# Packed attention with a gated layer on one core: w_out's first quarters loaded earlier, two output chunks started inside batch 0's h, output matmuls between batch 1's packed blocks

## The chip, the core and the metric

The kernel runs on one core of a Trainium2 chip. The metric is the device time of one execution in microseconds (us). All times below are of the kernel before the change, from three timed executions and one profiled execution with its trace.

The engines go by their profile names: PE (matmuls; PEld loads its weights), DVE (VectorE), ACT (ScalarE), POOL (GpSimd) and SP (SyncE). POOL and SP here mostly issue DMAs. Each engine works through its own instructions in program order and waits on semaphores of the others.

## The reference

```python
def _attn_ref(q, k, v, p):          # 8 batches, 8 heads, 576 tokens, head size 64; 32 packed queries p
    scale = 1.0 / np.sqrt(q.shape[-1])
    def sm_attn(qq, kk, vv):
        s = scale * np.matmul(qq, kk.transpose(0, 1, 3, 2))
        s = s - np.max(s, axis=-1, keepdims=True)
        a = np.exp(s)
        a = a / (np.sum(a, axis=-1, keepdims=True) + 1e-09)
        return np.matmul(a, vv)
    p_packed = sm_attn(p, k, v)
    return sm_attn(q, p_packed, p_packed)

def _moe_ref(x, w_in, w_out):       # x: 4608 x 512, w_in: 512 x 2048, w_out: 2048 x 512
    h = x @ w_in
    g = h * np.cos(h)
    return g @ w_out
```

The packed queries p attend to k and v; q attends to the result; the heads are joined to x, and x goes through the layer with w_in, h times cos(h), and w_out.

## The kernel before

One batch (576 tokens) after the other goes through these steps, and the steps of neighbouring batches are interleaved by an order written out by hand.

- `load` (L103) brings q, k or v of a batch, cast to bf16, by a DMA that POOL issues; `load_w_in` and `load_w_out` (L403, L407) bring a quarter of each weight matrix. POOL issues them in order, and at most eight are under way: the ninth waits until the first has landed.
- q and k are transposed, for batches 0 and 1 (and k of 2) by PE (`pe_T`, L119), later by DMAs on SP's queue (`xbar`, L111).
- `s1` (L160): scores of p and k on PE, exp on ACT, giving a1. a1 is transposed by PE (`a1_pe`, L181) or by a DMA on SP's queue (`a1_xbar`, L176), and `pp` (L191) multiplies it with v; `pp_T` (L206) transposes that to ppT.
- `s2` (L239): scores of q and pp, exp on ACT giving a2u; `sums2` (L246) sums on PE and takes Ln on ACT; `normalise` (L256) takes Exp on ACT and multiplies on DVE, giving a2n.
- `ppw` (L213): pp times w_in for 512 columns of w_in, the "packed block": eight matmuls on 64 rows and 32 columns of the array (L225). Four blocks make PPW of a batch. ACT and DVE copy them out, one bank each.
- h is a2n times PPW. It is made in 16 chunks of 128 of the 2048 columns. For batches 0 and 1, `h_one` (L295) makes 512 tokens of a chunk in one PSUM bank with two matmuls (L301); ACT takes the cosine (L306), DVE multiplies (L307) into gT. The last 64 tokens of eight chunks are made together by `h_half` (L310), which writes the tile joint. From batch 2 on, `h_mm` (L268) does all 576 tokens.
- The output: for each chunk of 128 tokens, 16 matmuls of gT with w_out accumulate in one bank (L365; for batch 0, L378), and `store` (L355) copies it to SBUF and has SP store it. These output matmuls are the filler: `fill(n)` (L395) emits the next n of them wherever the order says so. `out_first` (L371) gives the order for batch 0. It begins with the four matmuls on w_out's first quarter for each of the four chunks 0 to 3, and it keeps chunks 2 and 3 in two extra banks (psX).

PSUM has eight banks here. Two (pool O) hold output chunks. The other six are cut up in four ways (`banks`, L56): "pairs" are three tiles of two banks; "held" is psX with two banks, and two pairs; "single" is a ring of six single banks, H0 to H5, from which `one` (L115) takes the next by the counter `turn`; "four" is a ring of four single banks beside psX. When output chunk 3 of batch 0 is stored, `out_first` calls `banks("single")` and sets the counter: the ring then covers all six, psX's two as H0 and H1.

`slot(1, ...)` (L519, called at L563) is the h of batch 1: after each of the 16 chunks it emits its share of output matmuls (`weight`) and runs the hooks that stand at that chunk: the half chunks, transpositions on SP's queue, batch 1's fourth packed block.

The loads of later batches are tied to events by `behind` (L107): a POOL instruction that reads one element of a tile, so that what POOL issues after it waits until that tile is written.

Of the kernel before, what the change touches and what calls it, by code (L numbers as in the profile page):

```python
# [9 lines left out]
BF16 = mybir.dt.bfloat16  # L10
# [5 lines left out]
def kernel(  # L16
# [39 lines left out]
    def banks(kind):  # L56


        inner.close()
        if kind != "four":  # L60
            outer.close()
        for name, n, st in {"held": [("psX", 2, outer), ("psA", 1, inner)], "four": [("psH", 1, inner)],
                            "single": [("psH", 1, inner)]}.get(kind, [("psB", 1, inner), ("psA", 1, inner)]):
            psum[name] = st.enter_context(tc.tile_pool(name=name, bufs=n, space=PSUM, reuse_waits="tile"))
        pairs[:], turn[0] = (["A0", "A1"] if kind == "held" else ["A0", "A1", "B"]), 0
        ring[0] = 4 if kind == "four" else 6
        if kind in ("four", "single"):
            for i in range(ring[0]):
                psum["psH"].tile([128, 512], FP32, name="psH", tag=f"H{i}")
# [22 lines left out]
    def copy(eng, out, in_):  # L92
        if eng is ACT:
            ACT.copy(out=out, in_=in_)  # L94
        else:
            eng.tensor_copy(out=out, in_=in_)  # L96
# [10 lines left out]
    def behind(t):  # L107

        G.tensor_copy(out=gate, in_=t)  # L109
# [103 lines left out]
    def ppw(b, n, eng=None, own=None, later=False, cuts=((0, 512),)):  # L213
        if b not in PPW:
            PPW[b] = ppw_pool.tile([128, 2, DF], BF16, name="PPW", tag="PPW")
        two = isinstance(eng, tuple)
        if own:
            ps = [own(), own()]
        else:
            t = psa()  # L220
            ps = [t[:, 0, :], t[:, 1, :]]
        for x in range(4):
            for y in range(2):
                r = slice(64 * y, 64 * y + 64)
                nc.tensor.matmul(ps[y][32 * x:32 * x + 32, :], ppT[b % 2][r, 0, x, :],  # L225
                                 w_in_bf[r, x, n * 512:(n + 1) * 512], start=True, stop=True)

        def evacuate(cuts=cuts):
            if own or two:
                for a, z in cuts:  # L230
                    for y in range(2):
                        copy(eng[y] if two else eng, PPW[b][:, y, n * 512 + a:n * 512 + z], ps[y][:, a:z])
            else:
                copy(eng or (V, ACT)[n % 2], PPW[b][:, :, n * 512:(n + 1) * 512], t)
        if later:
            return [lambda c=c: evacuate((c,)) for c in cuts]
        evacuate()

    def s2(b):  # L239
# [67 lines left out]
            return lambda: V.tensor_tensor(out=gT[b][:, fc, 0:512], in0=ps, in1=cs, op=ALU.mult)  # L307
        return cos

    def h_half(b, a):  # L310

        t = one()
        for f in range(8):
            fc = 8 * a + f
            for y in range(2):
                nc.tensor.matmul(t[:, f * 64:f * 64 + 64], PPW[b][:, y, fc * 128:(fc + 1) * 128],  # L316
                                 a2n[b][:, y, 512:576], start=(y == 0), stop=(y == 1))
        cs = cos_pool.tile([128, 512], BF16, name="cosT")
        ACT.activation(out=cs, in_=t, func=AF.Sin, bias=PI_HALF)
        j0 = (b % 2) * 64  # L320
        V.tensor_tensor(out=joint[b // 2][:, 8 * a:8 * a + 8, j0:j0 + 64], in0=t.rearrange("p (f x) -> p f x", x=64),
                        in1=cs.rearrange("p (f x) -> p f x", x=64), op=ALU.mult)
# [46 lines left out]

    def out_first():  # L370

        pss = {}
        for c, fcs in ((0, 4), (1, 4), (2, 4), (3, 4), (0, 8), (1, 8), (2, 8), (3, 8),
                       (2, 12), (3, 12), (2, 16), (3, 16), (0, 16), (1, 16)):
            if c not in pss:
                pss[c] = (O if c < 2 else psum["psX"]).tile([128, DM], FP32, name="ot", tag="ot")
            for fc in range(8 if (c, fcs) in ((0, 16), (1, 16)) else fcs - 4, fcs):
                nc.tensor.matmul(pss[c], gT[0][:, fc, c * 128:(c + 1) * 128], w_out_bf[:, fc, :],  # L378
                                 start=(fc == 0), stop=(fc == NFC - 1))
                if fc == NFC - 1:  # L380
                    store(0, c, pss[c], V if c == 2 else ACT)
                    if c == 3:
                        banks("single")
                        turn[0] = 3
                yield

    filler = []

    def set_filler(b):
        filler.append([out_gen(b) if b else out_first(), 16 * n_chunks(b)])  # L390
# [12 lines left out]
    def load_w_in(n):  # L403
        G.dma_start(out=w_in_bf[:, :, n * 512:(n + 1) * 512],
                    in_=moe_w_in.rearrange("(a p) n -> p a n", p=128)[:, :, n * 512:(n + 1) * 512])

    def load_w_out(n):  # L407
        G.dma_start(out=w_out_bf[:, n * 4:(n + 1) * 4, :],
                    in_=moe_w_out.rearrange("(a p) n -> p a n", p=128)[:, n * 4:(n + 1) * 4, :])
# [15 lines left out]
    load("k", 1)  # L425
    for n in range(3):
        load_w_in(n)
    wz = const.tile([128, 512], BF16, name="wz")
    V.memset(wz, 0.0)
    wz4 = const.tile([128, 512], FP32, name="wz4")  # L430
# [21 lines left out]
    warm(1)  # L452
    pp_T(0)
    pe_T("q", 0, (V, ACT, V))
    load_w_out(0)
    load("q", 1)
    for n in range(1, 4):
        load_w_out(n)
    G.dma_start(out=p_raw[:, 4:, :], in_=p_rows[:, 4:, :])
    load("k", 2)  # L460
# [12 lines left out]
    cut_ppw()  # L473
    rest_ppw()
    banks("single")
    a1_pe(1, own=one)
    recips(1)
    for fc in range(13):
        h_one(0, fc)()()
        if fc in (0, 4, 8):  # L480
            ppw(0, 1 + fc // 4, (ACT, ACT if fc == 8 else V), own=bank)
    c13 = h_one(0, 13)
    pp(1, ACT, own=bank)
    c13()()
    c14 = h_one(0, 14)
    c15 = h_one(0, 15)
    pp_T(1, ACT, own=bank)
    c14()()
    c15()()
    set_filler(0)  # L490
    fill(4)
    for n, at in ((0, 2), (1, 0), (2, 4)):
        turn[0] = at
        if n == 2:
            fill(4)
            ACT.preload_act_table_set(EXP_SET)
        ppw(1, n, (ACT, V), own=one)
    banks("held")
    t = psa(BF16)
    for i in range(2):  # L500
        pe_T("q", 1, (None,) * 3, (i,), own=lambda dt: t[:, i, :])
    V.tensor_copy(out=xT["q", 1][:, 0:16].rearrange("p (i a) x -> p i (a x)", i=2), in_=t[:, :, 0:8 * TP])
    pe_T("q", 1, (V, V, ACT), (2,), own=lambda dt: psum["psX"].tile([128, 1024], dt, name="ot", tag="ot"))
    fill(4)
    load("k", 3)
    load("q", 2)
# [4 lines left out]
    sums2(1, 0)  # L511
    fill(2)
    sums2(1, 1)
    fill(9)
    normalise(1)
    ACT.preload_act_table_set(SIN_SET)
    fill(4)
# [40 lines left out]
    def cross(n, b):  # L558
        return lambda: xbar(n, b)

    osb_eng[0] = ACT
    banks("four")
    slot(1, [(5, lambda: h_half(0, 0)), (6, cross("k", 3)), (6, lambda: h_half(0, 1)),  # L563
             (7, lambda: ppw(1, 3, (ACT, V), own=one)), (9, cross("q", 2)), (9, lambda: h_half(1, 0)),
             (10, lambda: pack_p(2, 4, one(BF16))), (11, lambda: h_half(1, 1)), (12, tk2),
             (13, lambda: pe_T("k", 2, (None, None, V), (2,), own=one))],
         trail=8, heavy={5: (0, 1), 6: (0, 1), 7: (0, 1), 9: (0, 1), 11: (0, 1)},
         weight=[3, 3, 3, 4, 4, 2, 2, 2, 3, 2, 2, 2, 1, 2, 3, 3])
    banks("pairs")
    ACT.preload_act_table_set(EXP_SET)  # L570
    osb_eng[0] = V
    behind(xT["q", 2][0:1, 0, 0:1])
    load("v", 3)
    load("q", 3)
    load("k", 4)

    fill(4)
    s1(2)
# [6 lines left out]
    pp(2)  # L585
    s1(3)
    a1_xbar(3)
    fill(2)
    pp_T(2)
    recips(3)  # L590
# [13 lines left out]
    nc.sync.dma_start_transpose(out=P2[:, 4:B].rearrange("p b (t h) n -> p (b t) (h n)", t=2),  # L604
                                in_=p_bf[:, 8:2 * B].rearrange("p g t d -> p (g t d)"))
    behind(xT["k", 4][0:1, 0, 0:1])
    for n, b in (("v", 4), ("q", 4), ("k", 5)):
        load(n, b)
    fill(9)
    osb_eng[0] = ACT  # L610
    slot(2, [(7, lambda: tiled(2))], 0, {7: (6, 4)}, lambda: pp_T(3, V))
# [1 line left out]
    for s in range(3, B):  # L613
        nxt = s + 1 < B
        ACT.preload_act_table_set(EXP_SET)
        osb_eng[0] = V
        if s % 2:
            set_filler(s - 1)
        fill(5)
        s2(s)  # L620
        ppw(s, 0, V)
        fill(8 if nxt else 9)
        if nxt:
            s1(s + 1)
            ppw(s, 1, V)
            a1_xbar(s + 1)
            xbar("q", s + 1)
            recips(s + 1)
            if s + 2 < B:
                xbar("k", s + 2)  # L630
                behind(xT["k", s + 2][0:1, 0, 0:1])
        else:
            for n in range(1, 4):
                ppw(s, n, V)
        fill(4 if nxt else 5)
        sums2(s, 0)
        fill(5)
        sums2(s, 1)
        normalise(s)
        ACT.preload_act_table_set(SIN_SET)  # L640
        fill(13)
        osb_eng[0] = ACT
        for n, b in (("v", s + 2), ("q", s + 2), ("k", s + 3)):
            if b < B:
                load(n, b)
        if nxt:
            slot(s, [(7, lambda: tiled(s))], 0 if s % 2 else 1, {7: (5, 4)}, lambda: pp_T(s + 1, V),
                 7 if s % 2 else 0)
        else:
            slot(s, [], trail=7)  # L650
# [32 lines left out]
```

## Time and profile before

| | us |
|---|---|
| median of three executions (lowest, highest) | 244.16 (244.12, 244.28) |
| profiled execution, its own time | 244.22 |
| its span, first to last instruction | 242.4 |
| PE busy in the span | 232.9 |
| ACT, DVE, POOL busy | 166.5, 162.8, 36.2 |
| output matmuls (L365, L378, 128x512), mean of one | 0.38 |
| DMA queue of the loads (q0): moved | 18.75 MB |

How to read it: the span is what the trace covers, and the rest of the execution's time lies around it. A matmul's busy time is longer than the distance to the next, since matmuls overlap in the array, so a busy PE isn't yet PE at its peak. In the timeline, a row gives the start, the time from the first start to the last end, the engine, the line, the operation with output and inputs, the count, and in brackets the idle time of the engine ahead of it with what ended it. Rows of the same kind are merged. In the list of waits the three numbers are the total, the number of times and the longest.

### The profile page before, as it was taken

The numbers are of one execution on the slowest core, as the hardware profiler recorded it, in microseconds if no ns is written. First come the engines' busy times: TensorE is split into PE (matmuls) and PEld (weight loads), VectorE is DVE, ScalarE is ACT, GpSimd is POOL, SyncE is SP. The second block draws the span as 40 slices with busy tenths as digits, with TensorE's granted clock in tenths as the row PEclk, the third lists the DMA queues.
The fourth block names the chain that finished last, engine by engine and source line by source line (L and its number), as shares of the span: only waits on it lengthen the run. The fifth ranks groups of instructions, "written<-read, shape, count | busy, mean of one in ns | idle before, by whom it ended". The sixth has DMA issues, their size and how long they took to land.

```text
span 242.4 us, 5480 instructions
## 1 busy us (share of the span) xinstructions
PE 232.9 (96%) x2244; PEld 126.0 (52%) x2244; DVE 162.8 (67%) x261; ACT 166.5 (69%) x268; POOL 36.2 (15%) x58
## 2 busy tenths in 40 slices
PE   7789899999999999999999999999999999999994
PEld 3454244456445564556546554556456554565453
DVE  3259993688558786687857686777758787877001
ACT  2349899688659778876878677867787683776110
POOL 8522212200300005000500311030100110010000
PEclk9999999999999999999999999999999999999999
DMA  6999999999999999999999999989285101311133
GB/s 96 203 205 206 206 206 225 201 235 201 175 133 162 197 183 166 211 179 179 186 209 225 184 191 208 191 160 213 66 161 119 46 0 46 87 43 46 47 83 87
DMA packets 64376, 37.37 MB, mean 154 GB/s; under 512 B 36864, under 2 KB 59776, under 8 KB 64352
## 3 DMA queue, kind: packets, MB, share of 16 engines
q0 software_dynamic: 23152, 18.75, 51.7%
q1 hardware_dynamic: 40960, 18.16, 37.1%
q8 instruction: 17, 0.28, 0.5%
q10 hardware_dynamic: 240, 0.13, 0.2%
q14 instruction: 7, 0.06, 0.1%
HBM read 37.22 MB, written 9.44 MB: 192 GB/s over the span
## 4 chain that ended last, share of the span: by engine, by line
PE 83%; DMA 8%; DVE 4%; ACT 2%; issue 1%; POOLq 0%
PE ot L365 42%; PE psA L275 17%; PE ot L378 6%; DMA a1T<-a 5%; PE psH L301 4%; DMA kbf<-in_k_dram 3%; PE psA L155 2%; PE psA L225 2%; PE psA L251 2%; PE psA L198 1%; PE ot L348 1%; DVE gT L307 1%; DVE PPW L96 1%; PE psA L128 1%; PE psH L316 1%; DVE a2n L261 1%
## 5 line engine op out<-in xcount | busy, mean ns | idle before, releaser
L365 PE MATMUL ot<-w_out_bf,gT 128*128 128x512 bf16 x448 | 114.8, 379 | 0.0
L282 DVE TENSOR_TENSOR gT<-psA,cosT 128x576 bf16<-128x576 f32 x96 | 71.4, 757 | 16.3 <-ACT cosT L279 15.3
L279 ACT ACTIVATE cosT<-psA 128x576 bf16<-128x576 f32 x96 | 62.4, 652 | 21.3 <-PE psA L275 20.0
L275 PE MATMUL psA<-a2n,PPW 128*128 128x288 bf16 x384 | 62.7, 286 | 0.0
L365 PEld LDWEIGHTS <-gT 128*128 128x128 bf16 x448 | 42.1, 98 | 38.2 <-issue 4.2
L275 PEld LDWEIGHTS <-PPW 128*128 128x128 bf16 x384 | 37.5, 98 | 25.4 <-issue 0.6
L96 DVE CAST PPW<-psA 128x1024 bf16<-128x1024 f32 x19 | 23.0, 1220 | 7.9 <-PE psA L225 7.9
L307 DVE TENSOR_TENSOR gT<-psH,cosT 128x512 bf16<-128x512 f32 x32 | 21.0, 688 | 4.5 <-ACT cosT L306 4.4
L96 DVE COPY osb<-ot 128x512 f32<-128x512 f32 (+2 forms) x18 | 11.7, 649 | 16.1 <-PE ot L348 14.6
L306 ACT ACTIVATE cosT<-psH 128x512 bf16<-128x512 f32 x32 | 18.5, 615 | 4.6 <-PE psH L301 3.5
L94 ACT COPY osb<-ot 128x512 f32<-128x512 f32 (+1 forms) x20 | 11.4, 568 | 14.8 <-PE ot L365 12.2
L261 DVE SCALAR_TENSOR_TENSOR a2n<-a2u,r,lns 128x576 bf16<-128x576 bf16 x16 | 12.4, 815 | 12.4 <-ACT lns L259 12.4
L301 PE MATMUL psH<-a2n,PPW 128*128 128x512 bf16 x64 | 17.7, 380 | 1.0 <-DVE PPW L96 1.0
L378 PE MATMUL ot<-w_out_bf,gT 128*128 128x512 bf16 x64 | 17.8, 380 | 0.1
L286 POOL COPY joint<-gT 128x512 bf16<-128x512 bf16 x12 | 7.3, 616 | 64.6 <-DVE gT L282 64.6
L164 ACT ACTIVATE a<-psA 128x576 bf16<-128x576 f32 x16 | 10.3, 646 | 7.8 <-PE psA L155 7.8
L253 ACT ACTIVATE lns<-psA 128x576 f32<-128x576 f32 x16 | 10.4, 651 | 7.4 <-PE psA L251 6.8
L365 PE MATMUL ot<-w_out_bf,joint 128*128 128x512 bf16 x48 | 14.6, 379 | 0.0
L243 ACT ACTIVATE a2u<-psA,rs 128x576 bf16<-128x576 f32 x16 | 11.0, 737 | 1.4 <-PE psA L155 1.4
L109 POOL COPY gate<-kT 1x1 bf16<-1x1 bf16 x4 | 0.7, 178 | 74.4 <-DMA kT<-kbf 74.4
L301 PEld LDWEIGHTS <-PPW 128*128 128x128 bf16 x64 | 5.8, 98 | 8.3 <-DVE PPW L96 2.0
L259 ACT ACTIVATE lns<-lns 128x576 f32<-128x576 f32 x16 | 10.0, 673 | 0.0
(94 smaller groups left out, 197.0 us busy)
## 6 DMA issues: line engine op xcount, KB each, us to landing
kbf<-in_k_dram POOLq DMA_DIRECT2D x8, 576.0 KB, 14.6
vbf<-in_v_dram POOLq DMA_DIRECT2D x8, 576.0 KB, 8.7
qbf<-in_q_dram POOLq DMA_DIRECT2D x8, 576.0 KB, 11.5
out_dram<-osb SPq DMA_DIRECT2D x24, 192.0 KB, 2.8
out_dram<-osb SPq DMA_DIRECT2D x22, 128.0 KB, 2.5
w_in_bf<-in_moe_w_in_dram POOLq DMA_DIRECT2D x4, 512.0 KB, 17.0
w_out_bf<-in_moe_w_out_dram POOLq DMA_DIRECT2D x4, 512.0 KB, 21.1
out_dram<-osb SPq DMA_DIRECT2D x25, 64.0 KB, 2.7
```

Source lines behind the costliest of these rows:

```text
L94: ACT.copy(out=out, in_=in_)
L96: eng.tensor_copy(out=out, in_=in_)
L243: ACT.activation(out=a2u[b][:, y].rearrange("p (e x) -> p e x", e=2), in_=ps[y][:, :, 0:HS], func=AF.Exp, scale=rs1[b][:, y:y + 1])
L261: V.scalar_tensor_tensor(out=a2n[b][:, y], in0=a2u[b][:, y], scalar=r1[b][:, y:y + 1], in1=lns[b][:, y], op0=ALU.mult, op1=ALU.mult)
L275: nc.tensor.matmul(ps[:, e, 0:HS], PPW[b][:, y, fc * 128:(fc + 1) * 128], a2n[b][:, y, e * HS:(e + 1) * HS], start=(y == 0), stop=(y == 1))
L279: ACT.activation(out=csv, in_=ps[:, :, 0:HS], func=AF.Sin, bias=PI_HALF)
L282: V.tensor_tensor(out=gT[b][:, fc, :].rearrange("p (e x) -> p e x", e=2), in0=ps[:, :, 0:HS], in1=csv, op=ALU.mult)
L301: nc.tensor.matmul(ps, PPW[b][:, y, fc * 128:(fc + 1) * 128], a2n[b][:, y, 0:512], start=(y == 0), stop=(y == 1))
L306: ACT.activation(out=cs, in_=ps, func=AF.Sin, bias=PI_HALF)
L307: return lambda: V.tensor_tensor(out=gT[b][:, fc, 0:512], in0=ps, in1=cs, op=ALU.mult)
L365: nc.tensor.matmul(ps, w, w_out_bf[:, fc, :], start=(fc == 0), stop=(fc == NFC - 1))
L378: nc.tensor.matmul(pss[c], gT[0][:, fc, c * 128:(c + 1) * 128], w_out_bf[:, fc, :], start=(fc == 0), stop=(fc == NFC - 1))
```

## The change

Five places are edited:

1. **Loads.** w_out's first quarter is issued ahead of w_in's last quarter, and w_out's second quarter ahead of batch 1's q.
2. **h of batch 0.** Output chunks 0 and 1 start inside it: one output matmul behind each of the h chunks 8 to 11 and four behind chunk 12. Packed block 3 of batch 0 moves from behind chunk 8 to behind chunk 11 and is copied out in two cuts; the two half chunks of batch 0 move here from the slot of batch 1. `pp` and `pp_T` of batch 1 use the ring's banks instead of pool O's.
3. **Packed blocks of batch 1.** All four stand here now (the fourth was in the slot), with four output matmuls ahead of blocks 1 and 2. The table load for exp stands behind the fourth.
4. **Order of batch 0's output.** `out_first` takes the first half of chunks 0 and 1 first, then the first half of 2 and 3, then the second halves; the counter is set to 4 instead of 3 when chunk 3 ends. One output matmul less stands ahead of `normalise(1)`, and the slot of batch 1 has new weights and fewer hooks.
5. **Later loads.** q of batch 3 and k of batch 4 are issued only when a1 of batch 3 is written, and q of batch 4 and k of batch 5 only when a1 of batch 4 is.

```diff
     def ppw(b, n, eng=None, own=None, later=False, cuts=((0, 512),)):
...
-        two = isinstance(eng, tuple)
+        two = isinstance(eng, (tuple, list))
+        engs = eng if isinstance(eng, list) else [eng] * len(cuts)
...
-    def h_half(b, a):
+    def h_half(b, a, between=None):
...
+        if between:
+            between()
         cs = cos_pool.tile([128, 512], BF16, name="cosT")
...
     def out_first():
-        pss = {}
-        for c, fcs in ((0, 4), (1, 4), (2, 4), (3, 4), (0, 8), (1, 8), (2, 8), (3, 8),
-                       (2, 12), (3, 12), (2, 16), (3, 16), (0, 16), (1, 16)):
+        pss, at = {}, [0] * 4
+        for c, to in ((0, 4), (1, 4), (0, 8), (1, 8), (2, 8), (3, 8), (2, 16), (3, 16), (0, 16), (1, 16)):
...
                     if c == 3:
                         banks("single")
-                        turn[0] = 3
+                        turn[0] = 4
...
     for n in range(3):
         load_w_in(n)
+    load_w_out(0)
...
-    load_w_out(0)
+    load_w_out(1)
     load("q", 1)
-    for n in range(1, 4):
+    for n in range(2, 4):
         load_w_out(n)
...
     banks("single")
+    turn[0] = 4
     a1_pe(1, own=one)
     recips(1)
-    for fc in range(13):
+    set_filler(0)
+    for fc in range(12):
         h_one(0, fc)()()
-        if fc in (0, 4, 8):
-            ppw(0, 1 + fc // 4, (ACT, ACT if fc == 8 else V), own=bank)
-    c13 = h_one(0, 13)
-    pp(1, ACT, own=bank)
-    c13()()
+        if fc in (0, 4):
+            ppw(0, 1 + fc // 4, (ACT, V), own=bank)
+        if fc >= 8:
+            fill(1)
+    cut_ppw, rest_ppw = ppw(0, 3, [(ACT, ACT), (ACT, V)], own=one, later=True, cuts=((0, 128), (128, 512)))
+    cut_ppw()
+    h_half(0, 0, rest_ppw)
+    h_one(0, 12)()()
+    fill(4)
+    h_one(0, 13)()()
+    pp(1, ACT, own=one)
     c14 = h_one(0, 14)
     c15 = h_one(0, 15)
-    pp_T(1, ACT, own=bank)
     c14()()
+    pp_T(1, ACT, own=one)
     c15()()
-    set_filler(0)
-    fill(4)
-    for n, at in ((0, 2), (1, 0), (2, 4)):
-        turn[0] = at
-        if n == 2:
+    h_half(0, 1)
+    for n in range(4):
+        if n in (1, 2):
             fill(4)
-            ACT.preload_act_table_set(EXP_SET)
         ppw(1, n, (ACT, V), own=one)
+    ACT.preload_act_table_set(EXP_SET)
     banks("held")
+    fill(4)
...
-    pe_T("q", 1, (V, V, ACT), (2,), own=lambda dt: psum["psX"].tile([128, 1024], dt, name="ot", tag="ot"))
+    pe_T("q", 1, (V, V, ACT), (2,))
...
-    fill(9)
+    fill(8)
     normalise(1)
...
-    slot(1, [(5, lambda: h_half(0, 0)), (6, cross("k", 3)), (6, lambda: h_half(0, 1)),
-             (7, lambda: ppw(1, 3, (ACT, V), own=one)), (9, cross("q", 2)), (9, lambda: h_half(1, 0)),
-             (10, lambda: pack_p(2, 4, one(BF16))), (11, lambda: h_half(1, 1)), (12, tk2),
+    slot(1, [(5, lambda: h_half(1, 0)), (6, cross("k", 3)), (7, lambda: h_half(1, 1)), (9, cross("q", 2)),
+             (10, lambda: pack_p(2, 4, one(BF16))), (12, tk2),
              (13, lambda: pe_T("k", 2, (None, None, V), (2,), own=one))],
-         trail=8, heavy={5: (0, 1), 6: (0, 1), 7: (0, 1), 9: (0, 1), 11: (0, 1)},
-         weight=[3, 3, 3, 4, 4, 2, 2, 2, 3, 2, 2, 2, 1, 2, 3, 3])
+         trail=8, heavy={5: (0, 1), 7: (0, 1)}, weight=[3, 3, 3, 3, 3, 1, 2, 1, 2, 2, 2, 2, 1, 1, 2, 3])
...
     load("v", 3)
-    load("q", 3)
-    load("k", 4)
...
     a1_xbar(3)
+    behind(a1[1][0:1, 1, 0, 0:1])
+    load("q", 3)
+    load("k", 4)
...
     behind(xT["k", 4][0:1, 0, 0:1])
-    for n, b in (("v", 4), ("q", 4), ("k", 5)):
-        load(n, b)
+    load("v", 4)
...
             a1_xbar(s + 1)
+            if s == 3:
+                behind(a1[0][0:1, 1, 0, 0:1])
+                load("q", 4)
+                load("k", 5)
             xbar("q", s + 1)
```

More of the change, by code (lines that the diff above doesn't have):

```diff
@@ L226, in ppw, with evacuate @@
                                  w_in_bf[r, x, n * 512:(n + 1) * 512], start=True, stop=True)
-        def evacuate(cuts=cuts):
+        def evacuate(which=range(len(cuts))):
             if own or two:
-                for a, z in cuts:
+                for i in which:
+                    (a, z), e2 = cuts[i], engs[i]
                     for y in range(2):
-                        copy(eng[y] if two else eng, PPW[b][:, y, n * 512 + a:n * 512 + z], ps[y][:, a:z])
+                        copy(e2[y] if two else e2, PPW[b][:, y, n * 512 + a:n * 512 + z], ps[y][:, a:z])
             else:
@@ L235, in ppw @@
         if later:
-            return [lambda c=c: evacuate((c,)) for c in cuts]
+            return [lambda i=i: evacuate((i,)) for i in range(len(cuts))]
         evacuate()
@@ L370, in out_first @@
     def out_first():
-        pss = {}
-        for c, fcs in ((0, 4), (1, 4), (2, 4), (3, 4), (0, 8), (1, 8), (2, 8), (3, 8),
-                       (2, 12), (3, 12), (2, 16), (3, 16), (0, 16), (1, 16)):
+        pss, at = {}, [0] * 4
+        for c, to in ((0, 4), (1, 4), (0, 8), (1, 8), (2, 8), (3, 8), (2, 16), (3, 16), (0, 16), (1, 16)):
             if c not in pss:
                 pss[c] = (O if c < 2 else psum["psX"]).tile([128, DM], FP32, name="ot", tag="ot")
-            for fc in range(8 if (c, fcs) in ((0, 16), (1, 16)) else fcs - 4, fcs):
+            for fc in range(at[c], to):
                 nc.tensor.matmul(pss[c], gT[0][:, fc, c * 128:(c + 1) * 128], w_out_bf[:, fc, :],
@@ L383, in out_first @@
                         banks("single")
-                        turn[0] = 3
+                        turn[0] = 4
                 yield
+            at[c] = to
     filler = []
@@ L475 @@
     banks("single")
+    turn[0] = 4
     a1_pe(1, own=one)
     recips(1)
-    for fc in range(13):
+    set_filler(0)
+    for fc in range(12):
         h_one(0, fc)()()
-        if fc in (0, 4, 8):
-            ppw(0, 1 + fc // 4, (ACT, ACT if fc == 8 else V), own=bank)
-    c13 = h_one(0, 13)
-    pp(1, ACT, own=bank)
-    c13()()
+        if fc in (0, 4):
[9 more added lines that the diff above has]
+    pp(1, ACT, own=one)
     c14 = h_one(0, 14)
     c15 = h_one(0, 15)
-    pp_T(1, ACT, own=bank)
     c14()()
+    pp_T(1, ACT, own=one)
     c15()()
-    set_filler(0)
-    fill(4)
-    for n, at in ((0, 2), (1, 0), (2, 4)):
-        turn[0] = at
-        if n == 2:
-            fill(4)
-            ACT.preload_act_table_set(EXP_SET)
-        ppw(1, n, (ACT, V), own=one)
-    banks("held")
+    h_half(0, 1)
+    for n in range(4):
+        if n in (1, 2):
+            fill(4)
+        ppw(1, n, (ACT, V), own=one)
+    ACT.preload_act_table_set(EXP_SET)
+    banks("held")
+    fill(4)
     t = psa(BF16)
```

## The prediction

> **What bounds the kernel now.** I read the page's first two parts, then busy time by stretch, then what PE waited for, then single rows around each place that the change touches. The page says that PE is the bound, at full granted clock:
>
> ```profile
> PE 232.9 (96%) x2244; PEld 126.0 (52%) x2244; DVE 162.8 (67%) x261; ACT 166.5 (69%) x268; POOL 36.2 (15%) x58
> ...
> PE   7789899999999999999999999999999999999994
> ...
> PEclk9999999999999999999999999999999999999999
> ```
>
> By stretch (start:end, length, then busy time of PE, PEld, DVE, ACT, POOL, clock, DMA share, GB/s), PE has holes before 28 us and none from 36 to 63:
>
> ```profile
> 24.00:28.00 4.00, 2.99 (x19) 0.90 (x17) 4.00 (x8) 3.72 (x8) 1.66 (x2) 1.00 1.28 205
> 28.00:36.00 8.00, 7.95 (x117) 3.33 (x117) 7.60 (x14) 7.47 (x16) 0.93 (x2) 1.00 1.27 206
> 36.00:43.00 7.00, 7.00 (x61) 3.43 (x59) 2.99 (x4) 6.56 (x10) 1.53 (x2) 1.00 1.22 227
> 43.00:63.00 20.00, 20.00 (x177) 10.46 (x175) 15.93 (x25) 15.53 (x27) 1.59 (x2) 1.00 1.29 202
> ```
>
> So the end moves only by what PE waits less or more; PE work that is moved costs nothing. What PE waited for after its start is short (total, times, longest):
>
> ```profile
> PE psH L301 <- DVE PPW L96: 1.0, 2, 0.6
> PE psA L198 <- DMA a1T<-a: 0.5, 1, 0.5
> ```
>
> **The change, part by part.** Prices: an output matmul starts 0.216 after the one before (13 in 2.97 at L378, the last lasting 0.38: 2.59/12). A chunk of h is two of these, 0.43. A half chunk is 0.47 (L316 at 49.26, next matmul at 49.73). A packed block (ppw) is 0.34 (28.07 to 28.41) and about 0.09 of a later start behind full matmuls.
>
> *Up to chunk 8 of batch 0 nothing moves.* The same matmuls, copies and w_in quarters 0 to 2 come in the same order, so both PPW waits stay: the rows below show PE reaching chunks 4 and 8 at 24.76 and 27.75 behind DVE copies.
>
> ```profile
> 24.76 0.39 PE L301 MATMUL psH<-a2n,PPW 128*128 128x512 bf16 x1 [0.37 <-DVE PPW L96]
> ...
> 27.75 0.39 PE L301 MATMUL psH<-a2n,PPW 128*128 128x512 bf16 x1 [0.64 <-DVE PPW L96]
> ```
>
> *Chunk 8 to the first chunk of batch 1 (28 to 42.75).* Ahead of that chunk PE now does 42 output matmuls instead of 31 (2.38 us), batch 0's two half chunks (0.94) and the fourth packed block of batch 1 (0.4): 3.7 us, all taken out of the slot behind it. What counts is the waits.
>
> The loads: POOL saw w_in quarters land at 19.70, 22.23, 24.78 and 27.37 (its next issues), one per 2.6 us, and PE sees a landing about 0.35 earlier (w_out's first quarter is used at 32.53, as soon as it is there). w_out's first quarter takes the place of w_in's last, so that is seen at 29.6 and used at 30.2 (chunks 8 to 11 and four output matmuls, 10 x 0.216, lie before it); v of batch 1 at 32.6, used at 32.9; w_out's second quarter at 35.1, used at 35.5; q of batch 1 at 38.1, used at 39.4. Everything queued later on POOL keeps its place. No wait, with 0.3 to 0.6 to spare, and each late tenth would be paid.
>
> The engines: DVE works a gT per 0.60 without a gap (27.60 on), and PE's next chunks need only banks that are six tiles old. I find three small waits by following the copies: ppw(1,0) for ACT's copy of ppT, which now has a cos before it, 0.15; s2(1) for ACT's q copy behind the table load and four PPW copies, 0.2; and the first chunk of batch 1. That one needs a2n, 4.82 after a2u starts (38.13 to 42.95); PE has 18 instead of 19 output matmuls to put there, so 0.2. Before, PE lost about as much here: 0.1 for w_out at 32.5, 0.05 for q at 35.2, 0.2 for the q copy at 37.5 and 0.15 in the four bank waits of the double block at 33.5. Net 0.0; these being sums of tenths, -0.3 to +0.5. Output matmuls between the packed blocks therefore buy almost nothing: the blocks were not waiting long.
>
> *The ring of banks in batch 1's slot.* While output chunks 2 and 3 hold two banks, h runs on a ring of four (banks 2 to 5); when chunk 3 is finished, a ring of six over banks 0 to 5 begins at the number in turn. Before, chunk 3 ended behind h chunk 4 (bank 2) and the ring went on at 3, the oldest. Now 42 matmuls are done ahead of the slot, the weights give 2, 3, 2 behind chunks 0, 1, 2, so the 48th, chunk 3's last, is the first behind h chunk 2, which sits in bank 4, and the ring goes on at 4. Chunk 3 must wait until chunk 2 has been read; PE can do nothing else meanwhile. The built order agrees: chunk 3's first matmul waits for DVE, chunk 4 (bank 5) and chunk 5 (bank 0) for nothing new, the half chunk (bank 1) for ACT's copy of output chunk 3. The price, from batch 1's first chunk now:
>
> ```profile
> 42.75 0.63 PE L301 MATMUL psH<-a2n,PPW 128*128 128x512 bf16 x2
> ...
> 43.42 0.60 ACT L306 ACTIVATE cosT<-psH 128x512 bf16<-128x512 f32 x1 [0.18 <-PE psH L301]
> ...
> 44.05 0.69 DVE L307 TENSOR_TENSOR gT<-psH,cosT 128x512 bf16<-128x512 f32 x1 [1.10 <-ACT cosT L306]
> ```
>
> Second matmul at 42.97, cos at 43.42, gT from 44.05 to 44.74: 1.77; the release costs 0.06 more (copy ended 24.70, PE at 24.76). PE gets there itself after 0.22 for the second matmul and 0.43 for two output matmuls. 1.83 - 0.65 = **1.18** of idle PE. It can't be worth less than zero; a busy ACT or DVE would add up to one instruction (0.6), but both are shown waiting here (0.18, 1.10). I take 1.18.
>
> *The rest of the slot.* 30 instead of 41 output matmuls lie between the chunks: PE about 15.6 us, DVE 16 x 0.62 + 2 x 0.65 + copies = 13.2. From chunk 5 to 7, PE takes 3 x 0.43 + 2 x 0.47 + 3 x 0.22 = 2.9 and DVE 5 x 0.63 = 3.2, but six banks take up 0.3. Zero.
>
> *q of batch 3 and k of batch 4 behind a1 of batch 3.* Now:
>
> ```profile
> 65.73 0.77 POOL L105 DMA_DIRECT2D qbf<-in_q_dram  x1
> 66.50 0.77 POOL L105 DMA_DIRECT2D kbf<-in_k_dram  x1
> ...
> 70.14 4.72 SPq L178 DMA_TRANSPOSE a1T<-a  x1
> ...
> 83.48 0.56 PE L198 MATMUL psA<-vbf,a1T 96*32 96x64 bf16 x48 [0.46 <-DMA a1T<-a]
> ```
>
> The transposition of a1 lands 13.30 after its issue (chain of waits), 0.5 too late. By the tile view its five issues took 3.8, median 8.5 and at most 13.3. With the two loads issued only when it is, it has the queue alone for over a microsecond; I take about 8.5, since it still shares with the loads then: the wait goes, **-0.5** (0 to -0.53). *The Trainium skill, "DMA: Bandwidth & Descriptors", Queues, rings and completion order, says that each DMA engine goes round robin, packet by packet, between rings that have work. From 77 to 79 us the packet records agree (94 load and 94 transpose packets per 0.5 us); from 70.1 to 74.0 they don't, no transpose packet moves. By the rule alone the order of issue would matter little and this term would be 0, the sum 245.4.*
>
> Moved too: SP's k transposition (51.17) now stands behind chunk 0's two stores, some 4 us later, read at 68.4; q and k of later batches are asked for some 6 us later, read at 92.8 and 95.2, and POOL's gate for them stands ahead of joint copies read at 137.6. The k gate fell at 89.61, 5.6 before use. Nothing there waits unless all 6 us are lost. Zero, up to +1.
>
> **Sum.** The profiled execution took 244.22 (span 242.4 and 1.8 around it), 0.06 over the median of 244.16. 244.22 + 0.0 + 1.18 - 0.5 = 244.9; against the median **244.85**.
>
> **Rivals.**
> - *A: the bank wait isn't there* (not slower). If the ring of six lay otherwise over the banks than I infer, chunk 3 would find a bank read long ago; from a bank two chunks old on, the wait is under 0.1. Then 244.16 - 0.5 + 0.0 to -0.3 = 243.4 to 243.7. For it: no view shows bank numbers. Against: every wait in the built order fits. 0.12.
> - *B: a1T still comes late*, the two loads taking its packets as before: 245.35. For it: 13.30 with loads queued; against: they are now queued after it. 0.17. *By the Trainium skill's rule above this is what comes.*
> - *C: the later loads come too late*, and s1(4) waits for k: decides from 5.6 us on; about 246. 0.08.
> - *D: the stretch from 28 us gains*: none of my three waits appears and the old ones go, 0.4 to 0.5 better: 244.4. 0.15.
> - *E: forecast*, 244.5 to 245.2: 0.48.
>
> **Numbers.** The range takes in B, D and E with their tenths: 243.8 to 245.7; A and C are left out (0.2). 0.2%, about what a measurement of this kernel can tell from no change, is 0.49: faster is below 243.67, A's larger part, 0.11; same to 244.65 is D, the low end of E and the rest of A, 0.27; slower 0.62.
>
> **What would show it.** PE idle of about 1.2 at L303 (h chunk of batch 1, some 50 us in), released by DVE's gT: if absent, A. The idle before L198 near 84 gone: if not, B. PE's two waits at 24 and 27 unchanged. Batch 1's first chunk at 46.4 to 46.9: earlier is D. PE waiting for a DMA between 30 and 40 would mean that my landing times are off by more than 0.3; at s2(3) or s1(4), C.

## The result and the profile after

The changed kernel takes **244.82 us** (median of 7 runs, 244.46 to 245.09); the kernel before 243.77 (median of 7: the three executions above, 244.12 to 244.28, and four later ones, 243.62 to 243.77). The ratio is 1.0038, 95% interval 1.0028 to 1.0047, or +0.93 us (+0.68 to +1.15); it isn't the ratio of the two medians, which lie 1.05 apart. The forecast was 244.85. The profiled execution took 244.52, with a span of 242.7.

The page's engine row and the two lines of PE's waits that matter, after the change:

```profile
PE 229.0 (94%) x2209; PEld 125.8 (52%) x2244; DVE 163.1 (67%) x262; ACT 166.1 (68%) x269; POOL 36.8 (15%) x60
```

```profile
PE psH L303 <- DVE PPW L96: 1.0, 2, 0.6
PE psH L303 <- DVE gT L309: 1.0, 1, 1.0
```

The first wait is the old one ahead of the second matmuls of chunks 4 and 8 of batch 0. The second is new. The old wait for a1T before L198 is gone. Read the engine row with care: PE appears 4 us less busy, but it has 2209 matmul records where PEld has 2244 weight loads. 35 records are missing. Each leaves a hole of one matmul's pitch (0.216) in the row of starts, and up to 0.16 of it looks like idle time. So busy time by stretch is a poor guide here (start:end, length, busy time of PE, PEld, DVE, ACT, POOL, clock, DMA share, GB/s):

```profile
28.00:36.00 8.00, 7.89 (x123) 4.03 (x123) 7.48 (x13) 7.07 (x17) 0.87 (x2) 1.00 1.29 204
36.00:43.00 7.00, 6.89 (x84) 3.27 (x85) 4.13 (x7) 5.50 (x9) 1.53 (x2) 1.00 1.23 228
43.00:63.00 20.00, 18.83 (x137) 9.70 (x138) 14.49 (x23) 15.91 (x27) 1.82 (x2) 1.00 1.31 202
```

In the last row 1.17 is not busy, and most of it is real. From one start to the next, PE's own rows show where:

```profile
47.53 0.81 PE L381 MATMUL ot<-w_out_bf,gT 128*128 128x512 bf16 x3
48.17 0.59 PE L303 MATMUL psH<-a2n,PPW 128*128 128x512 bf16 x2
48.60 0.59 PE L381 MATMUL ot<-w_out_bf,gT 128*128 128x512 bf16 x2
50.18 0.59 PE L303 MATMUL psH<-a2n,PPW 128*128 128x512 bf16 x2 [0.98 <-DVE gT L309]
```

The two matmuls of chunk 2 start at 48.17 and 48.39, two output matmuls follow at 48.60 and 48.82, and chunk 3 starts at 50.18 instead of 49.04: 1.14 lost. DVE shows what it waited for, the gT of chunk 2:

```profile
49.44 0.69 DVE L309 TENSOR_TENSOR gT<-psH,cosT 128x512 bf16<-128x512 f32 x1 [0.39 <-ACT cosT L308]
```

It ends at 50.13, and PE goes on 0.05 later. Ahead of that, the second matmul of chunk 8 starts at 27.71 (27.75 before), and batch 1's first chunk starts at 45.98. Behind it, the fourth product of a1 and v starts without a wait:

```profile
83.78 0.56 PE L198 MATMUL psA<-vbf,a1T 96*32 96x64 bf16 x48
```

Between the first trace of before and this one, PE gains 0.04 up to chunk 8 and 0.22 up to batch 1's first chunk, loses 1.14 at the bank, gains 0.46 at a1T and 0.12 in pieces of a few hundredths: +0.3, as the profiled executions differ. (The 0.22 is 3.71 of work moved ahead, at the prediction's prices, less the 3.49 by which the stretch between the second matmuls of the two chunks got longer.) But the timed runs differ by 0.93. The experiments had to explain that 0.6 as well.

### The profile page after: what moved, and what is told of

The parts are those of the page before. It is cut to its first block, busy times and chain, and to the rows that moved or that the text cites. A ratio compares the mean times of both kernels' runs of the same rounds, so it can differ in the third digit from the quotient of the medians.

```text
span 242.7 us, 5454 instructions
## 1 busy us (share of the span) xinstructions
PE 229.0 (94%) x2209; PEld 125.8 (52%) x2244; DVE 163.1 (67%) x262; ACT 166.1 (68%) x269; POOL 36.8 (15%) x60
## 4 chain that ended last, share of the span: by engine, by line
PE 86%; DVE 5%; DMA 3%; ACT 3%; issue 2%; POOLq 0%
PE ot L369 43%; PE psA L277 19%; PE ot L381 4%; PE psH L303 4%; DMA kbf<-in_k_dram 3%; PE psA L226 2%; PE psA L155 2%; PE psA L253 2%; DVE gT L309 2%; PE ot L352 1%; PE psA L198 1%; DVE a2n L263 1%; PE psA L128 1%; DVE PPW L96 1%; PE psH L318 1%
## 5 line engine op out<-in xcount | busy, mean ns | idle before, releaser
L369 PE MATMUL ot<-w_out_bf,gT 128*128 128x512 bf16 x424 | 109.7, 379 | 2.0 <-issue 1.6
L303 PE MATMUL psH<-a2n,PPW 128*128 128x512 bf16 x62 | 18.2, 380 | 2.2 <-DVE PPW L96 1.0
L381 PE MATMUL ot<-w_out_bf,gT 128*128 128x512 bf16 x61 | 17.0, 380 | 0.1
L164 ACT ACTIVATE a<-psA 128x576 bf16<-128x576 f32 x16 | 10.2, 646 | 7.8 <-PE psA L155 7.8
L369 PE MATMUL ot<-w_out_bf,joint 128*128 128x512 bf16 x45 | 14.0, 379 | 0.3 <-issue 0.2
```

The lines of the kernel that those rows point to most:

```text
L303: nc.tensor.matmul(ps, PPW[b][:, y, fc * 128:(fc + 1) * 128], a2n[b][:, y, 0:512], start=(y == 0), stop=(y == 1))
L369: nc.tensor.matmul(ps, w, w_out_bf[:, fc, :], start=(fc == 0), stop=(fc == NFC - 1))
```

## The experiments

Kernels of one group ran on the same chip, with runs of the kernel before between theirs (86 of them in the three groups that were timed, medians 243.77 to 243.84). *Theory*: the loss is the bank wait alone, 1.1, less 0.2 gained before it; the wait for a1T is in some executions of before only, the first profiled one among them, so removing it brings the median nothing. *Rivals*: the bank wait only stands in for a later wait; or the loss comes from the later loads.

**ring5: the ring's number alone**

```diff
                     if c == 3:
                         banks("single")
-                        turn[0] = 4
+                        turn[0] = 5
```

> The changed kernel, with one number other: when output chunk 3 is finished, the ring of six banks goes on at 5 instead of 4, so h chunk 3 of batch 1 takes a bank whose reader is long done. Theory (the bank wait is a loss on the path): PE's idle time of 1.0 before h chunk 3 goes, nothing of its size appears behind it, and the time falls by 1.0 to 1.2 against the changed kernel, to about 243.7, as fast as before or up to 0.3 faster. Rival 1 (PE is ahead of something else in this stretch: the bank wait only stands in for a later wait): the idle time goes and comes back at a later bank, half chunk or at s1(2), and the time falls by less than 0.4. Rival 2 (the loss of 0.9 comes from the later loads and stores, not from the bank): time unchanged at 244.8.

243.83, ratio to before 0.9993 (0.9984 to 1.0001), -0.17 us. PE's rows at the same place:

```profile
48.33 0.59 PE L303 MATMUL psH<-a2n,PPW 128*128 128x512 bf16 x2
48.77 0.59 PE L381 MATMUL ot<-w_out_bf,gT 128*128 128x512 bf16 x2
49.20 0.59 PE L303 MATMUL psH<-a2n,PPW 128*128 128x512 bf16 x2
```

Chunk 3 follows after 0.87, with no wait, and s1(2) starts at 62.91, counted from chunk 8 1.13 earlier than in the changed kernel: nothing comes back. One digit is the whole loss, and the rest of the change is worth -0.17 (-0.39 to +0.02).

**before_again: the kernel before, unchanged**

> The kernel before, unchanged, for a second profile of it: its first one had a wait of 0.46 for the transposition of a1 of batch 3, 13.3 us after its issue, and was itself 0.45 longer than the fastest runs of the same kernel. Theory (the transposition's landing varies from one execution to the next, and only some executions wait for it): time 243.6 to 244.3; in this profile the landing need not be 13.3, and with no wait the execution is 0.3 to 0.5 shorter than the first profiled one. Rival (the wait is there in every execution): landing near 13 and a wait of 0.4 to 0.5 again.

Median 244.16 of 12 runs, ratio to the other runs of before 1.0018 (1.0000 to 1.0036): a kernel against itself can be off by this much. The profiled execution took 244.42, and its waits are others than in the first one:

```profile
PE ot L225 <- DMA w_in_bf<-in_moe_w_in_dram: 0.9, 3, 0.4
PE ot L378 <- DMA w_out_bf<-in_moe_w_out_dram: 0.9, 1, 0.9
```

No wait for a1T: its transposition lands 11.6 after its issue (13.3 in the first profile). The view of its issue gives the duration of the issuing instruction on SP in ns, and the landing:

```profile
L178 SPq DMA_TRANSPOSE a1T<-a x1: 4026/4026/4026, 70.9 to 70.9; - x1
DMA to landing us min/median/max: 11.6/11.6/11.6
```

PE wants a1T 12.8 after the issue, here as in the other traces. So a1T's wait is a matter of the execution, and so are waits for the weights.

**before_loads_behind_a1: the later loads alone**

```diff
     load("v", 3)
-    load("q", 3)
-    load("k", 4)
 ...
     a1_xbar(3)
+    behind(a1[1][0:1, 1, 0, 0:1])
+    load("q", 3)
+    load("k", 4)
```

(and the same for q of batch 4 and k of batch 5.)

> The kernel before with one part of the change alone: the loads of q of batch 3 and k of batch 4 (and of q of 4, k of 5) issued behind the transposition of a1. My forecast's term: the wait for a1T goes, 0.5 less than before, 243.3 to 243.7 where before stands at 243.8 to 244.2. Rival (the wait is only in some executions): the landing falls below 10 in the profile, and the times of the rounds move by less than 0.2, since the median execution of before does not wait there.

243.86, ratio 0.9997 (0.9989 to 1.0006), -0.07 us. The landing comes 6.1 after the issue, which is the mechanism that I forecast; the time stays. My -0.5 is outside the interval (-0.27 to +0.15).

```profile
L178 SPq DMA_TRANSPOSE a1T<-a x1: 1448/1448/1448, 70.6 to 70.6; - x1
DMA to landing us min/median/max: 6.1/6.1/6.1
```

The issuing instruction itself takes 1.4 here and 4.0 in before_again, which is about half of the difference. In return a later transposition, that for batch 5, lands later: issued at 123.2, after 10.2 here, and after 9.0 to 10.9 in all seven traces with the loads behind, against 3.9 to 8.5 in the seven with the loads ahead. PE waits for it in none of them.

**after_loads_ahead: the change without that part**

The same edit the other way round, in the changed kernel.

> The changed kernel with those loads put back where they were ahead of the change, before s1(2). Forecast's term: a1T is late again, 0.4 to 0.5 more than the changed kernel, about 245.3. Rival (in most executions there was no such wait to be removed): 244.7 to 244.9, within 0.2 of the changed kernel; what the profile shows of the landing (8 to 13 us) decides between a chance execution and the rule.

244.61, ratio to before 1.0031 (1.0019 to 1.0042), against 1.0038 for the whole change. The landing is at 11.0 again, and nobody waits. The part does what it says to the transfer and nothing to the time.

**before_third: a third profile of the kernel before**

> The kernel before, unchanged, for a third profile of it. Its two profiled executions so far took 244.22 and 244.42, above its median of 243.8, and each had a wait for a load that the other had not (a1T 0.5; w_in and w_out 1.0 to 1.8). Theory (where a load lands varies from one execution to the next, and the median execution waits little): if this execution takes 243.6 to 243.9, its waits for w_in, w_out, q and a1T add up to 0.3 at most; if it takes 244.1 or more, to 0.5 or more. Rival (the executions differ elsewhere): the same waits at either time.

This execution took 243.81, the median of the other groups. The only wait for a load on its list is that for the first k (0.9), which every trace has (0.3 to 1.9); ahead of w_out's first quarter PE is idle for 0.13, against 0.05 in the first profile and 0.93 in the second, and a1 lands after 10.5. So an execution of before that waits little for loads takes 243.8. The first profiled one took 0.41 longer: it was 0.08 ahead when it came to s1(2) and lost 0.49 behind that, 0.46 of it at a1T. Here are chunk 8 and s1(2), in this trace and then in the changed kernel's:

```profile
27.83 0.39 PE L301 MATMUL psH<-a2n,PPW 128*128 128x512 bf16 x1 [0.64 <-DVE PPW L96]
...
63.14 0.44 PE L155 MATMUL psA<-kT,P 64*32 64x288 bf16 x16
```

```profile
27.71 0.39 PE L303 MATMUL psH<-a2n,PPW 128*128 128x512 bf16 x1 [0.64 <-DVE PPW L96]
...
63.89 0.44 PE L155 MATMUL psA<-kT,P 64*32 64x288 bf16 x16
```

From one to the other PE takes 35.31 here and 36.18 in the changed kernel: **+0.88**, which is +1.14 at the bank and -0.26 for all the rest of the change (of that, 0.22 up to batch 1's first chunk). It lies within the runs' interval (+0.68 to +1.15), which is too wide to check it closer. By their own times the two executions differ by 0.71 only: the changed kernel's came to chunk 8 0.13 earlier, and gained 0.04 behind s1(2). By the medians (244.82, and 243.81 as here) the kernels lie 1.0 apart, the first two profiles 0.3: the 0.7 that was missing is the 0.41 by which the first profile lies above the median of before, and the 0.30 by which the profiled execution of the changed kernel (244.52) lies under its own.

**before_ring2: the same wait put into the kernel before**

```diff
-                        turn[0] = 3
+                        turn[0] = 2
```

> The kernel before with one number other: when output chunk 3 is finished, the ring of six goes on at 2 instead of 3, so h chunk 5 of batch 1 takes the bank that chunk 4 has just used. The wait is put into the kernel that didn't have it, at another place: four output matmuls lie between there, not two. Theory (the price is the time from a chunk's second matmul to its gT's release, less the work that PE has meanwhile): 0.22 + 4 x 0.216 = 1.08 instead of 0.65 of cover, so 1.14 - 0.43 = 0.7 of idle time before chunk 5, and 0.6 to 0.8 more than before, about 244.5. Rival (the changed kernel's 0.9 has another cause and the bank wait costs next to nothing): within 0.2 of before.

244.48, ratio 1.0024 (1.0015 to 1.0032), +0.59 us (0.37 to 0.78).

```profile
47.30 0.59 PE L301 MATMUL psH<-a2n,PPW 128*128 128x512 bf16 x2
47.74 1.03 PE L378 MATMUL ot<-w_out_bf,gT 128*128 128x512 bf16 x4
49.31 0.59 PE L301 MATMUL psH<-a2n,PPW 128*128 128x512 bf16 x2 [0.55 <-DVE gT L307]
```

Chunk 4's second matmul starts at 47.52, chunk 5 at 49.31: 1.79 until the bank is free, the same as in the changed kernel (48.39 to 50.18). There 0.65 of it was covered, here 1.08, so 0.71 is lost (the runs' +0.59 has it in its interval). The chain took the same time at both places; what a wrong number costs depends on how many output matmuls lie behind the chunk.

**before_load_order: the order of the weight loads alone**

```diff
     for n in range(3):
         load_w_in(n)
+    load_w_out(0)
 ...
-    load_w_out(0)
+    load_w_out(1)
     load("q", 1)
-    for n in range(1, 4):
+    for n in range(2, 4):
```

> The kernel before with the load order of the change alone: w_out's first two quarters ahead of w_in's last and of batch 1's queries, all matmuls where they were. By the landings that the changed kernel shows, w_in's last quarter comes at 29.6 where PE wants it at 28.1 (wait 1.5), v of batch 1 at 32.6 (wanted at 32.3 by then: 0.3), q at 38.1, wanted near 36.7 (1.2 to 1.5): some 2.7 more than before, about 246.5. Theory: the order of loads is a loss by itself, and pays only because the output matmuls were moved up to where PE would wait. Rival (DVE's queue, which is full to 36 us, sets the pace there, and PE's waits for loads are hidden behind it): under 1.0 more, below 244.8.

246.59 (four runs, 245.97 to 247.07), ratio 1.0109 (1.0092 to 1.0126), +2.66 us. The terms stand where they were put, but are sized otherwise:

```profile
30.39 0.41 PE L225 MATMUL ot<-w_in_bf,ppT 64*32 64x512 bf16 x8 [2.27 <-DMA w_in_bf<-in_moe_w_in_dram]
...
33.35 0.56 PE L198 MATMUL ot<-vbf,a1T 96*32 96x64 bf16 x48 [0.28 <-DMA vbf<-in_v_dram]
...
38.72 0.47 PE L128 MATMUL psA<-ident,qbf 96*128 96x96 bf16 x7 [1.01 <-DMA qbf<-in_q_dram]
```

2.27, 0.28 and 1.01, some of which covers waits that were there before. Of the 2.27, some 0.8 is this execution's: w_in's last quarter lands at 30.34 here and at 29.54 in the changed kernel's trace. The load order is a loss by itself. In the changed kernel packed block 3, which needs that quarter, stands behind three more chunks and four output matmuls and isn't reached before 30.18; no run tells the move of the block from the output matmuls.

**after_fill9: one output matmul more ahead of the slot**

```diff
     sums2(1, 1)
-    fill(8)
+    fill(9)
     normalise(1)
```

> The changed kernel with 9 instead of 8 output matmuls ahead of normalise, ring number 4 left as it is. The 48th output matmul then falls behind h chunk 1 (bank 3), so that 4 is the oldest bank and the number is right by place; and one more matmul covers the chain to a2n. Theory: the bank wait of 1.0 is gone without touching the number, the 0.25 between the two matmuls of batch 1's first chunk falls to about 0.05, and the time is 1.1 to 1.4 under the changed kernel, 243.4 to 243.7. Rival (only the number mattered by chance, or a2n's wait moves elsewhere): bank wait gone and a2n's 0.2 shows up as another wait in the slot, 243.8. Rival 2 (bank wait is not the loss): 244.6 to 244.8.

243.26, ratio to before 0.9984 (0.9971 to 0.9997): 1.3 less than the changed kernel by the two ratios. Against before the interval only just leaves out 1; the two kernels built on this one, below, are clearer. The ring's number is untouched. The 48th output matmul now ends behind chunk 1, so 4 is the right number, and the matmul covers a2n too (first chunk's two matmuls 0.25 apart instead of 0.465). Its trace also shows how little the loads have to spare in the changed order. In this execution v of batch 1 lands at 33.12 (32.44 in the changed kernel's trace), and PE waits for it where it didn't there:

```profile
PE psH L198 <- DMA vbf<-in_v_dram: 0.2, 1, 0.2
```

**after_no_waits: every wait covered, a miss**

```diff
                     if c == 3:
+                        newest = 2 + (turn[0] - 1) % ring[0]
                         banks("single")
-                        turn[0] = 4
+                        turn[0] = newest + 1
 ...
+    fill(1)
     s2(1)
 ...
-    fill(8)
+    fill(9)
     normalise(1)
```

> The changed kernel with three edits: the ring of six goes on behind the newest bank, worked out where it starts; 9 instead of 8 output matmuls ahead of normalise; one more ahead of s2(1). Theory: bank wait 1.14 gone, a2n's wait 0.25 gone, s2's wait for the copy of q (0.18) gone; 1.4 to 1.6 under the changed kernel, 243.2 to 243.5, and 0.4 under before. Rival (the two matmuls taken out of the slot were cover there, and as much is lost again): 243.6 to 243.9, as the kernel with the ring number alone.

245.00, ratio to before 1.0075 (1.0044 to 1.0105; three of its nine runs took 247.0 to 247.7): by the medians 1.2 slower than before and 1.7 slower than after_fill9, and neither theory nor rival had that. DVE and then PE:

```profile
45.40 0.69 DVE L96 COPY osb<-ot 128x512 f32<-128x512 f32 x1 [4.72 <-PE ot L381]
46.01 2.42 DVE L263 SCALAR_TENSOR_TENSOR a2n<-a2u,r,lns 128x576 bf16<-128x576 bf16 x2
```

```profile
47.19 0.38 PE L303 MATMUL psH<-a2n,PPW 128*128 128x512 bf16 x1 [0.97 <-DVE a2n L263]
48.48 0.38 PE L303 MATMUL psH<-a2n,PPW 128*128 128x512 bf16 x1 [0.92 <-DVE a2n L263]
```

With one more output matmul ahead of normalise, the 40th, output chunk 2 is finished there, and its copy to osb stands ahead of a2n in DVE's queue. DVE sits idle for 4.72 and waits for PE's 40th matmul, while the inputs of a2n's first half are there: ACT's exp for it ends at 44.68. (In the changed kernel that exp ends at 44.82 and a2n starts at 44.85.) a2n starts 1.16 later than there and then takes 2.42 instead of 1.55; PE waits for it twice, 1.13 and 1.08 by start to start.

**no_waits_a2n_first: the same order on PE, two instructions exchanged on DVE**

```diff
-    fill(9)
+    fill(8)
     normalise(1)
     ACT.preload_act_table_set(SIN_SET)
-    fill(4)
+    fill(5)
```

> The kernel after_no_waits, which came out 1.2 slower than before, with normalise issued one output matmul earlier in the program: TensorE's order is the same to the last instruction, and on DVE only one pair changes places, a2n now ahead of the copy of finished output chunk 2. Theory: that copy, which must wait for the 40th output matmul, held DVE's queue and so a2n, which PE then waited for twice (1.1 and 1.1 in that trace); with a2n first both waits go, 1.7 to 2.2 less, about 243.0 to 243.3, and the waits for a2n and for ACT's copy of q before s2 are gone as well. Rival (it is the 44 matmuls taken out of the slot, or the later s2, that cost): still 244.5 to 245.

243.00, ratio to before 0.9981 (0.9959 to 1.0004; the interval is wide since two of its 12 runs took 244.8 and 245.8). By the medians it is 2.0 under after_no_waits, which ran in another group (before took 243.82 here and 243.77 there). a2n is first now, and PE's first chunk of batch 1 has next to no wait left (its two matmuls start 0.25 apart):

```profile
44.89 1.55 DVE L263 SCALAR_TENSOR_TENSOR a2n<-a2u,r,lns 128x576 bf16<-128x576 bf16 x2 [4.04 <-ACT lns L261]
46.35 0.69 DVE L96 COPY osb<-ot 128x512 f32<-128x512 f32 x1
```

That a2n was held up by the copy is thus shown, with PE's order the same to the last instruction. By median this is the fastest kernel of the study; that it beats after_fill9 (another chip) is not shown, since the intervals overlap.

**fill9_loads_ahead and fill9_cut_copies: two further waits, taken away from after_fill9**

The first has the later loads back ahead of s1(2); the second cuts two copies:

```diff
-            ppw(0, 1 + fc // 4, (ACT, V), own=bank)
+            ppw(0, 1 + fc // 4, (ACT, V), own=bank, cuts=((0, 128), (128, 512)))
```

> The kernel after_fill9 (the changed kernel with 9 output matmuls ahead of normalise) with the later loads back ahead of s1(2), as in the kernel before. Theory: the wait for a1T depends on how early PE gets to the fourth product of a1 and v; in after_fill9 that is 82.8, a little ahead of where it was in the first profile of before (82.96), and the landing with loads ahead came at 82.0 to 83.4: a wait of 0 to 0.5, some 0.2 in the median, 243.3 to 243.6. Rival 1 (the part is worth its 0.5 always): 243.7 to 243.8. Rival 2 (it is worth nothing, as in the kernel before): 243.2 to 243.3.

> The kernel after_fill9 with the copies of batch 0's packed blocks 1 and 2 cut at column 128, as those of blocks 0 and 3 are, so that chunks 4 and 8 wait for a quarter of a copy. PE's two waits there (0.4 and 0.6, both before and after the change) get shorter. Theory: nothing is gained, since DVE is full up to 36 us and w_in's last quarter, v and w_out land at the same time as before, and in the trace of after_fill9 PE already waits 0.5 in all for them: waits for loads take their place, 243.2 to 243.5. Rival (PE's waits are what they seem): 0.5 to 1.0 less, 242.3 to 242.8.

243.22, ratio 0.9976 (0.9966 to 0.9985), and 243.32, ratio 0.9978 (0.9968 to 0.9987); after_fill9 had 0.9984. Neither moves the time. In the first, a1 lands after 10.9 and PE doesn't wait. PE comes to that product at 82.45, half a microsecond earlier than in the first profile of before, but the transposition is issued as much earlier (69.63): PE wants a1T 12.8 after the issue again, so the theory's premise, that an earlier PE waits more, was wrong. In the second, PE waits less for the copies and more for the loads:

```profile
PE psH L303 <- DVE PPW L96: 0.3, 1, 0.3
PE ot L226 <- DMA w_in_bf<-in_moe_w_in_dram: 0.3, 1, 0.3
```

Counted from batch 0's first chunk, and against fill9_loads_ahead, whose code is the same up to here but for the cut, PE is at chunk 4 0.42 earlier (2.62 and 3.04), waits 0.32 for w_in's third quarter behind it, is at chunk 8 0.36 earlier, waits 0.14 more at the fourth packed block (for w_in's last quarter) and 0.26 ahead of chunk 12 (for a copy of that block on ACT), and comes to batch 1's first chunk 0.16 later (24.69 and 24.53). But this execution's loads land later too: w_in's third quarter at 24.97, 3.19 behind the first chunk, against 24.45 and 2.77 in fill9_loads_ahead. So the median shows that the cut gains nothing; that waits for loads take the place of those for the copies in every execution isn't shown.

## Why the prediction was right, and where not

- **Up to chunk 8 nothing moves: right.** Both waits are unchanged (0.36 and 0.64 where 0.37 and 0.64 were).
- **Chunk 8 to batch 1's first chunk, net 0.0 (-0.3 to +0.5): a little too high.** 0.22 gained. The waits came where I put them, for ppT 0.16 (forecast 0.15) and for a2n 0.25 (0.2); the third, for the q copy, is as before. No load was waited for there. The chunk came at 45.98 where I had 46.4 to 46.9: 0.2 of it is this gain, and 0.25 that a2n's wait stands behind the chunk's first matmul, not ahead of it. By the sign that I gave, this was rival D; but D had none of my three waits and 0.4 to 0.5 gained, and all three waits are there with half of that.
- **The ring's number, +1.18: right.** 1.14 measured, since the release takes 1.79, not 1.83: in the rows that I worked it out from, the second matmul starts at 43.00 (42.75 + 0.63 - 0.38), not at 42.97. ring5 takes it out, before_ring2 puts it in, after_fill9 makes the number right by moving the place. Rival A is out.
- **a1T, -0.5: the step that failed.** The mechanism held: the landing fell from 13.3 to 7.2. But PE wants a1T some 12.8 after that issue, and of six traces with the loads issued ahead, only the one I forecast from has a later landing (13.3; the others 10.5 to 11.6). The median execution had nothing to give. Rival B is out too, for the transfer does come earlier. With the loads behind it, a1 landed after 6.1 to 7.2 in the five traces that have the landing. Two parts of the difference can be told apart: SP's issuing instruction took 3.7 to 4.7 with the loads ahead and 1.4 to 2.5 with them behind (seven traces each), and from its end to the landing it was 6.6 to 8.6 against 4.5 to 5.3. *The Trainium skill, "DMA: Bandwidth & Descriptors", Queues, rings and completion order, says how a DMA engine chooses between rings that have work, round robin by packets. That the order of issue would matter little was my conclusion from it, and the traces are against the conclusion; the rule itself says nothing of the time that issuing takes, and the 4 us without a transpose packet, which I held against it, fall within SP's issuing instruction (70.14 to 74.86). The term of 0 that I worked out from it was right all the same, for another reason: PE has the time to spare. The sum of 245.4 was not, since it started from the execution that had the wait.*
- **The rest, 0: right**, C is out: s1(4) and s2(3) wait for no load.
- **The sum.** That the time came out within 0.03 is luck: two errors cancelled. I took 0.5 off a profiled execution of 244.22 that had the wait, and set it against a median of 244.16 from three runs; 86 more runs put that median 0.35 lower, at about 243.8, where an execution without the wait lies. So 244.85 was right for the changed kernel, and the difference that I forecast, +0.7, was 0.2 too small: it should have had +1.14 and -0.2, without the -0.5.

What stays open: what sets the landing of a load from one execution to the next. No view shows it, and two of the three profiled executions of before had waits that its median execution, by its time, has not. Open too is why SP's issuing instruction takes longer with the loads ahead, and which of the other edits make up the 0.2 gained.

## What to carry to other kernels

When a change moves the point where PSUM banks are laid out anew, recompute from which bank the ring goes on: here one digit cost 1.1 us, and all the rest of the change was worth 0.2 (by the timed runs 0.17, not clear of zero). Before a matmul is moved up to cover a wait, look at what it finishes: the copy of its result enters another engine's queue at that place, and held the very operand that was to be covered. And a wait seen in one profiled execution is worth its price only if that execution's time is the median's; profile the kernel twice and set each against the timed runs.

## What the runs showed of the hardware that was not expected

- Where a load lands differs by execution. PE was idle for 0.05, 0.93 and 0.13 ahead of w_out's first quarter in three executions of the same kernel, and the a1 transposition took 13.3, 11.6 and 10.5.
- DVE and POOL took turns. In after_no_waits the two a2n multiplications took 1.13 and 1.37 (0.82 in the changed kernel), and POOL's casts of p beside them 0.82 and 1.35. Their ends alternate: POOL 46.52, DVE 47.14, POOL 47.82, DVE 48.43, each 0.61 to 0.69 behind the other's. DVE's copy from PSUM beside the same cast kept its 0.69. *The Trainium skill, "SBUF — State Buffer", SBUF: two separate sides, says that an operation of DVE with two SBUF inputs and one of GpSimd that reads SBUF exclude each other for a whole instruction; these rows agree.*
